# Two attention layers on one core: each row-maximum operation is declared to the planner as a writer of its whole accumulator bank, and the planner gets a new table of offsets

## The chip, the cores and the metric

The kernel runs on one core of one Trainium2 chip. The metric is device time in microseconds (us): the median of three runs of the kernel before is 1676.51 us (1674.89 to 1676.59).

## The reference

Two layers of the same size (sequence 2048, width 1024, 32 heads of 32) are computed in float32, and their outputs stand side by side. Layer A goes over four segments of 512 tokens. In each it does causal softmax attention inside the segment and reads a memory of the earlier segments; layer B is a linear attention with a learned feature map.

```python
# layer A, segment s (qs, ks, vs: heads x 512 x 32)
logits = einsum("bhqd,bhkd->bhqk", qs, ks) * scale + mask     # mask: -1e9 above the diagonal
a_dot = softmax(logits) @ vs
a_mem = phi(qs) @ M / (phi(qs) @ z + 1e-6)                    # phi(t) = t + 1 if t > 0 else exp(t)
outs.append(g * a_mem + (1 - g) * a_dot)
M, z = M + phi(ks)^T vs, z + sum(phi(ks))
a = concat_heads(outs) @ wo
# layer B
phi_x = concat(softmax(x @ w_phi), softmax(-x @ w_phi))       # for x = q and x = k
b = concat_heads(phi_q @ (phi_k^T v) / (phi_q @ sum(phi_k) + 1e-6)) @ wo
out = concatenate([a, b], axis=-1)
```

## The kernel before

Products that need float32 accuracy are made of three float16 products: each operand is split into a high and a low half, and high x high, high x low and low x high are accumulated in one bank of the accumulator memory (PSUM, eight banks of 128 x 512 float32).

**Attention (layer A, to about 880 us).** The work is cut into 32 units, u = 0 to 31: one segment and one group of four heads each. `produce(u)` projects keys, queries and values (PE, L496), splits them (ACT L938, DVE L940) and copies the halves by DMA into a tile `S` (three in turn). `attend(u)` then does the following.

- *Maxima.* For softmax a row maximum is needed for each of 4 heads h and 4 blocks i of 128 query rows. Block i sees 128·(i+1) keys, so the score products are 128 to 512 columns wide. `maxima` (L991 to L1007) takes a bank of kind `s`, has PE write the products of one or two blocks into it (L999), and has DVE add the causal mask and take the maximum over each block's columns (L1005, in the trace `CUSTOM_DVE_ANT_0` with an accumulator read behind it; the result lands in a column of `mt`). Per head, (h,3) has a bank of its own (512 columns), (h,2) and (h,0) share one (384 and 128 columns), and for each two heads (h−1,1) and (h,1) share one (256 and 256). That makes 16 maxima in 10 banks a unit, 512 in all.
- *Their way into the scores.* POOL makes `mh` and `mr` from all 16 columns of `mt` (L1020 to L1022), PE turns them into rows (L1024), ACT copies these (L1026), and DMAs put them into the tile `S` as eight extra rows, so that the second score product (L1104) comes out with the maximum taken off.
- *Softmax and output.* ACT takes the exponential and the high half (L1108, L1110), DVE the low half (`ph`, L1111), POOL masks (L1117), PE multiplies by the values (`pv`, L1140), DVE sums (`oall`, L1144) and scales, PE transposes (L1172), ACT copies (`oT`, L767).

Beside it the weights of layer B are folded (L1245, L1248) and split. **Layer B** follows with products by Strassen's method (L710), then the output projections (L496 and L1805).

**What sets the order.** Nothing is issued while the program's operations are named. Each is recorded with its engine, an assumed duration, a due time `prio`, and the tiles that it reads (`r`) and writes (`w`). A write can name a part of a tile by a key: `(ps, i)` is part i of the bank, `ps` alone is all of it. Two operations depend on each other if they touch the same part or if one touches the whole. The planner (`Graph.run`) then goes through an imagined time: it takes the engine that can start something first, and on it, among the operations whose dependencies are done at that moment, the one with the smallest due time. A dependency of DVE on DVE adds 0.13 us in that imagined time. What comes out is the order of the instructions on each engine; each engine runs its own in that order and waits on semaphores for the others. These waits come from the tiles that the instructions really touch, not from the keys.

`MOVES` is a table by engine. Operations named in a row with the same due time are a job, numbered from 0, and the table adds an offset to the due time of one engine's operations of one job:

```python
prio += MOVES.get(eng, {}).get(self.job[1], 0.0)
```

Of the kernel before, what the change touches and what calls it, by code (L numbers as in the profile page):

```python
# [383 lines left out]
def tile_kernel(ctx: ExitStack, tc: tile.TileContext, ax, aw, awv, awo, beta, bx, bwqk, bwv, bphi, bwo, out):  # L384
# [68 lines left out]
    for t in mhp:  # L453
# [9 lines left out]
       w=[gates], prio=0.2, lat=2.0, kb=16)  # L463
# [284 lines left out]
    def group(u):  # L748
# [4 lines left out]
       w=[(stk[0], (1, 3))], prio=0.3)  # L753
    for t in stk[1:]:
        op(SP, 0.6, lambda t=t: nc.sync.dma_start(t()[96:104, 1], stk[0]()[96:104, 1]), r=[(stk[0], (1, 3))],
           w=[(t, (1, 3))], prio=0.3, lat=1.6, kb=32)
# [213 lines left out]
    def attend(u):  # L970
# [18 lines left out]
        mt = G.buf("a", [128, 4, 4], F32, "mt", 2)  # L989

        def maxima(*blocks):  # L991
            ps = bank("s", [128, 512], "maxima")
# [43 lines left out]
        if s > 0:  # L1036
            amem = G.buf("a", [128, 4, 4, 32], F32, "amem", 1)
            for b in range(2):
                ps = bank("misc", [128, 2, 4, 33], "memory")
# [837 lines left out]
```

## Time and profile before

| | |
|---|---|
| median of three runs | 1676.51 us (1674.89 to 1676.59) |
| the profiled execution's own time | 1675.73 us |
| its span, first to last instruction | 1674.0 us |
| mean granted TensorE clock | 0.997 of full speed |
| instructions | 40119 |
| moved by DMA | 299.18 MB, mean 179 GB/s |

A row of the timeline has the start and the duration in us, then engine, line, operation and tiles (out<-in); what stands in brackets is the idle time before it and who ended it. Durations of products on PE overlap: the next product starts before the duration of the last is over, so the distance of two starts is what a product costs. The same holds for DVE, where the accumulator read behind a maximum starts before the maximum's duration is over. A row of waits has the engine and line that waited, whom it waited for, the sum in us, how often, and the longest.

### The profile page before, as it was taken

The page shows a single profiled execution, that of the slowest core. Times are in us where ns is not written, and L with a number is a line of the kernel's source. Part 1 is how long each engine was busy: PE and PEld are TensorE (multiplying, and loading weights), DVE is VectorE, ACT ScalarE, POOL GpSimd, SP SyncE. Part 2 cuts the span into 40 slices and gives each one's busy share as a digit, 9 for nine tenths or more (in the row PEclk, how much of TensorE's full clock was granted, in tenths as well). Part 3 has the DMA queues.
Part 4 walks back from the last instruction along what each step waited for, and adds up shares of the span by engine and source line. Part 5 has one row for each costly group of instructions (what it writes and reads, how often), then busy time and mean ns, then how long its engine had stood idle before and what let it go on. Part 6 is the DMA issues. An engine that isn't in the chain of part 4 may idle for free.

```text
span 1674.0 us, 40119 instructions
## 1 busy us (share of the span) xinstructions
PE 1633.2 (98%) x14964; PEld 963.1 (58%) x14964; DVE 1355.2 (81%) x3187; ACT 1120.9 (67%) x2096; POOL 1062.9 (63%) x1453
## 2 busy tenths in 40 slices
PE   8999999999999999999999999999979999999999
PEld 6666756766676676667665444445534444444444
DVE  6999899998998877798874898778999888964451
ACT  7789979795978878678744676766445555543341
POOL 4667878866689988778541767636478897730000
PEclk9999999999999999999999999999989999999999
DMA  6866765787866576755457364467546768872321
GB/s 211 224 175 151 250 185 169 226 212 191 229 166 210 154 197 210 200 172 157 104 159 274 123 223 164 154 219 283 195 101 166 182 171 183 212 181 99 108 88 69
DMA packets 291410, 299.18 MB, mean 179 GB/s; under 512 B 169088, under 2 KB 222336, under 8 KB 284560
## 3 DMA queue, kind: packets, MB, share of 16 engines
q1 hardware_dynamic: 291216, 296.63, 61.1%
q8 instruction: 117, 1.92, 0.5%
q14 instruction: 77, 0.63, 0.1%
HBM read 161.17 MB, written 86.05 MB: 148 GB/s over the span
## 4 chain that ended last, share of the span: by engine, by line
PE 43%; DVE 5%; ACT 1%; DMA 1%; POOL 0%; issue 0%; DVEq 0%; ACTq 0%
PE proj L710 17%; PE misc L496 9%; PE proj L1805 5%; PE s L710 3%; PE s L1805 2%; PE misc L710 2%; PE misc L1805 1%; PE kv L1556 1%; DVE mx L1395 1%; PE pv L1746 1%; DMA pt<-S 1%; DVE S L1734 1%; DVE pt L1549 1%; DMA wf_d<-oT 0%; DVE r L1405 0%; DVE s L1005 0%
## 5 line engine op out<-in xcount | busy, mean ns | idle before, releaser
L496 PE MATMUL proj<-S,S 128*128 128x128 f16 (+1 forms) x3072 | 500.5, 299 | 2.8 <-ACT S L529 1.2
L496 PEld LDWEIGHTS <-S 128*128 128x128 f16 x4608 | 327.7, 97 | 152.7 <-issue 9.8
L710 PE MATMUL proj<-S,S 128*128 128x512 f16 x1584 | 365.2, 380 | 3.9 <-ACT cs L716 2.4
L710 PEld LDWEIGHTS <-S 128*128 128x128 f16 x2016 | 192.5, 98 | 224.1 <-issue 7.8
L1111 DVE SCALAR_TENSOR_TENSOR ph<-s,ph 128x512 f16<-128x512 f32 x320 | 210.4, 682 | 50.6 <-ACT ph L1110 48.3
L1005 DVE CUSTOM_DVE_ANT_0 s<-s,causal 128x512 f32<-128x512 f32 (+3 forms) x512 | 240.9, 513 | 8.8 <-PE s L999 5.0
L1117 POOL TENSOR_SCALAR_AFFINE_SELECT ph<-ph 128x256 f16<-128x256 f16 (+1 forms) x448 | 195.1, 458 | 76.6 <-DVE ph L1111 58.5
L1110 ACT ACTIVATE ph<-s 128x512 f16<-128x512 f32 x320 | 191.9, 657 | 1.3 <-POOL fo L609 0.4
L496 PE MATMUL misc<-S,ot 128*128 128x512 f16 x768 | 172.2, 379 | 0.0
L1402 ACT ACTIVATE e<-e,sk 128x256 f32<-128x256 f32 x256 | 112.4, 496 | 67.0 <-DVE e L1399 64.2
L496 PEld LDWEIGHTS <-ot 128*128 128x128 f16 x768 | 73.5, 98 | 87.2
L1104 PE MATMUL s<-S 104*128 104x512 f16 (+3 forms) x512 | 117.0, 299 | 2.7 <-DVE amem L1049 0.7
L999 PE MATMUL s<-S 96*128 96x512 f16 (+3 forms) x512 | 111.2, 299 | 3.4 <-ACT pk L952 1.0
L1108 ACT ACTIVATE s<-s,os 128x512 f32<-128x512 f32 x160 | 105.7, 705 | 12.8 <-PE s L1104 12.7
L1108 ACT ACTIVATE s<-s,bd 128x512 f32<-128x512 f32 x160 | 108.0, 721 | 2.5 <-PE s L1104 2.4
L496 PE MATMUL proj<-wv,S 128*128 128x128 f16 x1536 | 108.2, 219 | 0.4 <-DVE ph L1111 0.4
L1140 PEld LDWEIGHTS <-ph 128*128 128x128 f16 x2560 | 87.8, 96 | 20.5 <-issue 2.8
L1140 PE MATMUL pv<-vl,ph 128*128 128x66 f16 (+1 forms) x2560 | 92.3, 184 | 1.5 <-ACT pk L952 0.7
L1405 DVE TENSOR_REDUCE r<-e 128x32 f32<-128x1024 f32 x64 | 76.7, 1207 | 18.0 <-ACT e L1402 17.9
L1710 POOL TENSOR_TENSOR e<-e,zb 128x512 f32<-128x512 f32 x62 | 82.5, 1350 | 12.4 <-ACT zb L1582 7.2
L1005 DVE DVE_READ_ACCUMULATOR2_ANT mt<- 128x1 f32 x512 | 72.4, 141 | 0.0
L1514 POOL TENSOR_TENSOR e<-e,r 128x1024 f32<-128x1024 f32 x32 | 62.1, 1943 | 14.4 <-DVE r L1408 10.0
(345 smaller groups left out, 3259.9 us busy)
## 6 DMA issues: line engine op xcount, KB each, us to landing
S<-xf_d SPq DMA_DIRECT2D x126, 256.0 KB
S<-h SPq DMA_DIRECT2D x192, 128.0 KB
S<-wf_d SPq DMA_DIRECT2D x21, 1024.0 KB
st<-bwqk SPq DMA_DIRECT2D x64, 256.0 KB
out<-os SPq DMA_DIRECT2D x40, 256.0 KB
S<-aw SPq DMA_DIRECT2D x16, 512.0 KB
wa_d<-S SPq DMA_DIRECT2D x16, 512.0 KB
wf_d<-fo SPq DMA_DIRECT2D x32, 256.0 KB
```

What stands on the lines that cost most here:

```text
L496: op(PE, dur, lambda c=c, a=a, b=b, lv=lv, rv=rv: nc.tensor.matmul(pv(), lv(), rv(), start=(c == 0 and a + b == 0), stop=(c == n - 1 and a ...
L710: op(PE, 0.215, lambda n=n, a=a, b=b, lv=lv, rv=rv: nc.tensor.matmul(ps(), lv(), rv(), start=(start and n == 0 and a + b == 0), stop=(n == ...
L999: nc.tensor.matmul(ps()[:, o:o + 128 * i + 128], st()[0:96, 0, h, 128 * i:128 * i + 128], st()[0:96, 1, h, 0:128 * i + 128], start=True, s ...
L1005: dve(0.073 + 0.001125 * n, lambda h=h, i=i, o=o, n=n: nc.vector.tensor_tensor_reduce(ps()[:, o:o + n], ps()[:, o:o + n], causal[:, 512 - ...
L1104: nc.tensor.matmul(ps()[:, o:o + n], st()[0:104, 1, h, 128 * j:128 * j + 128], st()[0:104, 0, h, 128 * j:512], start=True, stop=True)
L1108: act(0.59, lambda: nc.scalar.activation(ps(), ps(), AF.Exp, bias=0.0, scale=bdv()[:, 3, i2, 0:1]), r=[(bd, i2)], w=[ps])
L1110: act(0.48, lambda: nc.scalar.activation(ph()[:, 0], ps(), AF.Copy, scale=2.0 ** 14), r=[ps], w=[(ph, 0)])
L1111: dve(0.6, lambda: nc.vector.scalar_tensor_tensor(ph()[:, 1], ps(), 2.0 ** 14, ph()[:, 0], op0=OP.mult, op1=OP.subtract), r=[ps, (ph, 0)], ...
L1117: nc.gpsimd.affine_select(pd, pd, pattern=[[0, n], [1, 128]], compare_op=OP.is_ge, fill=0.0, base=0, channel_multiplier=-1)
L1140: nc.tensor.matmul(ps()[:, i, n0:n1], ph()[:, a, o:o + 128], vl()[:, j, h, n0:n1], start=(i == 0 and a == 0), stop=(j == min(i, 2)), skip_ ...
L1402: op(ACT, 0.41, lambda i=i: nc.scalar.activation(e()[:, 4 * i:4 * i + 4], e()[:, 4 * i:4 * i + 4], AF.Exp, bias=0.0, scale=sk()[:, i:i + 1 ...
L1805: op(PE, 0.215, lambda n=n, a=a, b=b: nc.tensor.matmul(ps(), v(a)[:, n, :], wform[w]()[:, b, n, :], start=(start and n == 0 and a + b == 0 ...
```

## The change

Each maximum is declared as a writer of `ps`, the whole bank, instead of part i of it. In the planner the second maximum of a bank thus depends on the first also where their numbers i differ: in 128 pairs, (h,2) and (h,0) of each head and unit. The pairs (h−1,1) and (h,1) had equal keys and depended on each other before. The table `MOVES` is replaced; a line of it is shown. For jobs above 209 only a few offsets differ. No operation, duration, tile or DMA is added or removed. The new table has one line fewer, so each line of the code behind it has a number smaller by one (L1005 is L1004).

```diff
 MOVES = {
     "DVE": {
-        0: -8.8, 4: -25.3, 7: 1.6, 8: -0.7, 10: -2.9, 12: -20.2, 13: 24.6, 14: -1.3, 15: -10.6, 16: -16.6, 17: 0.6, 18: 0.7,
...
+        0: 0.8, 4: -24.4, 8: 1.2, 9: -0.9, 10: -1.2, 12: -18.7, 13: 72.6, 14: 9.7, 16: 16.9, 17: 53.7, 18: 0.3, 19: 0.8,
...
                 dve(0.073 + 0.001125 * n, lambda h=h, i=i, o=o, n=n: nc.vector.tensor_tensor_reduce(
                     ps()[:, o:o + n], ps()[:, o:o + n], causal[:, 512 - n:512], 1.0, NEG, OP.add, OP.max,
-                    mt()[:, h, i:i + 1]), w=[(mt, (h, i)), (ps, i)])
+                    mt()[:, h, i:i + 1]), w=[(mt, (h, i)), ps])
```

The order moves on all engines: 6129 of PE's 9476 operations, 1705 of DVE's 2666, 1269 of ACT's 2011, 1003 of POOL's 1438 and 655 of SP's 1033 stand in another place than before. Two places show what moves.

DVE, the last maxima of unit u = 14, before. The first name is the bank (`s_` and its number), the last part the width; the row with `mt` alone is the accumulator read.

```order
L1005 ISA s_7306,mt_7225<-s_7306,causal_82 128x512
L1005 ISA mt_7225 128x1
L1005 ISA s_7321,mt_7225<-s_7321,causal_82 128x384
L1005 ISA mt_7225 128x1
L1005 ISA s_7321,mt_7225<-s_7321,causal_82 128x128
L1005 ISA mt_7225 128x1
L1005 ISA s_7333,mt_7225<-s_7333,causal_82 128x256
L1005 ISA mt_7225 128x1
L1005 ISA s_7333,mt_7225<-s_7333,causal_82 128x256
```

The same place with the change:

```order
L1004 ISA s_7819,mt_7751<-s_7819,causal_82 128x512
L1004 ISA mt_7751 128x1
L1004 ISA s_7813,mt_7751<-s_7813,causal_82 128x128
L1004 ISA mt_7751 128x1
L1004 ISA s_7828,mt_7751<-s_7828,causal_82 128x384
L1004 ISA mt_7751 128x1
L1004 ISA s_7865,mt_7751<-s_7865,causal_82 128x256
L1004 ISA mt_7751 128x1
L1004 ISA s_7828,mt_7751<-s_7828,causal_82 128x128
L1004 ISA mt_7751 128x1
L1004 ISA s_7865,mt_7751<-s_7865,causal_82 128x256
```

Before, the two maxima of a bank (384 and 128 wide of s_7321, 256 and 256 wide of s_7333) stand directly behind each other; now a maximum of another bank stands between them. Over the kernel, 105 of the 128 pairs (h,2), (h,0) and 3 of the 64 pairs (h−1,1), (h,1) stand directly behind each other before, and 2 and 0 with the change.

PE, just ahead of the product that turns the maxima of the same unit into rows (L1024 before, L1023 with the change), before. `proj` is a projection of a later unit.

```order
L496 LDWEIGHTS S10_5648
L496 MATMUL proj_7326<-S5_5604,S10_5648 128x512
L1024 LDWEIGHTS mh0_126
L1024 MATMUL misc_7369<-identr_89,mh0_126 128x128
L496 LDWEIGHTS S10_5648
L496 MATMUL proj_7326<-S5_5604,S10_5648 128x512
```

With the change:

```order
L495 LDWEIGHTS S10_5624
L495 MATMUL proj_7822<-S5_5209,S10_5624 128x512
L998 LDWEIGHTS S12_135
L998 MATMUL s_7907<-S12_135 128x256
L998 LDWEIGHTS S12_135
L998 MATMUL s_7907<-S12_135 128x256
L1023 LDWEIGHTS mh0_126
L1023 MATMUL misc_7910<-identr_89,mh0_126 128x128
```

Before, sixteen projection products stand between the unit's last maxima product and L1024. With the change nine projection products and eight maxima products of the next unit, 128 to 512 columns wide, stand there.

## Rows read from the trace of the kernel before

**Rows 1.** The page: busy us of each engine (share of the span) x instructions.

```profile
PE 1633.2 (98%) x14964; PEld 963.1 (58%) x14964; DVE 1355.2 (81%) x3187; ACT 1120.9 (67%) x2096; POOL 1062.9 (63%) x1453
```

**Rows 2.** Busy time by stretch (us): length, engines (x), clock, DMA; last L1005 alone.

```profile
0.00:41.00 41.00, 36.69 (x287) 27.81 (x287) 27.05 (x73) 29.49 (x49) 18.45 (x34) 1.00 0.68 208
...
41.00:880.00 839.00, 819.72 (x8893) 564.20 (x8894) 738.43 (x2132) 671.56 (x1237) 636.90 (x1003) 1.00 0.67 187
...
900.00:1290.00 390.00, 377.26 (x2777) 185.84 (x2776) 324.84 (x558) 235.44 (x482) 239.78 (x234) 0.99 0.58 188
...
1210.00:1240.00 30.00, 18.39 (x164) 7.85 (x164) 29.93 (x52) 13.99 (x29) 22.11 (x23) 0.84 0.47 98
...
1290.00:1674.00 384.00, 379.56 (x2841) 174.36 (x2839) 252.26 (x404) 169.39 (x302) 160.20 (x166) 1.00 0.53 144
...
41.00:880.00 839.00, 254.88 (x1024) 1.00 0.67 187
```

**Rows 3.** Waits of PE, 40 to 900 us: sum, times, longest.

```profile
PE misc L1024 <- POOL mh L1022: 3.6, 8, 1.2
...
PE misc L1024 <- DVE wgs L511: 0.9, 1, 0.9
...
PE s L999 <- DMA S<-h: 0.8, 1, 0.8
...
PE misc L881 <- DVE xam L575: 0.2, 1, 0.2
```

**Rows 4.** Timeline of DVE, the end of the maxima of unit u = 14.

```profile
403.76 0.14 DVE L1005 DVE_READ_ACCUMULATOR2_ANT mt<- 128x1 f32 x1
403.94 0.30 DVE L1005 CUSTOM_DVE_ANT_0 s<-s,causal 128x128 f32<-128x128 f32 x1
...
404.15 0.73 DVE L1005 CUSTOM_DVE_ANT_0 s<-s,causal 128x512 f32<-128x512 f32 x1
...
404.80 0.60 DVE L1005 CUSTOM_DVE_ANT_0 s<-s,causal 128x384 f32<-128x384 f32 x1
405.32 0.14 DVE L1005 DVE_READ_ACCUMULATOR2_ANT mt<- 128x1 f32 x1
405.49 0.30 DVE L1005 CUSTOM_DVE_ANT_0 s<-s,causal 128x128 f32<-128x128 f32 x1
...
405.71 0.46 DVE L1005 CUSTOM_DVE_ANT_0 s<-s,causal 128x256 f32<-128x256 f32 x1
406.09 0.14 DVE L1005 DVE_READ_ACCUMULATOR2_ANT mt<- 128x1 f32 x1
406.27 0.43 DVE L1005 CUSTOM_DVE_ANT_0 s<-s,causal 128x256 f32<-128x256 f32 x1
406.62 0.14 DVE L1005 DVE_READ_ACCUMULATOR2_ANT mt<- 128x1 f32 x1
```

**Rows 5.** Timeline of DVE, a pair of maxima with a small operation between.

```profile
106.43 0.60 DVE L1005 CUSTOM_DVE_ANT_0 s<-s,causal 128x384 f32<-128x384 f32 x1
...
106.94 0.22 DVE L1227 SCALAR_TENSOR_TENSOR twf<-twf,phs 128x1 f32<-128x1 f32 x1
107.12 0.30 DVE L1005 CUSTOM_DVE_ANT_0 s<-s,causal 128x128 f32<-128x128 f32 x1
```

**Rows 6.** Timeline of PE, u = 14: what follows its last maxima product, and L1024.

```profile
403.83 3.62 PE L496 MATMUL proj<-S,S 128*128 128x512 f16 x16
408.65 0.23 PE L1024 MATMUL misc<-identr,mh 128*128 128x128 f16 x1 [1.20 <-POOL mh L1022]
```

**Rows 7.** Timeline of POOL in the same place.

```profile
406.92 0.26 POOL L1020 TENSOR_SCALAR mh<-mt 128x16 f16<-128x16 f32 x1 [1.68 <-DVE mt L1005]
...
408.04 0.56 POOL L1022 TENSOR_TENSOR mh<-mr,mt 128x16 f16<-128x16 f32 x1
```

**Rows 8.** Timeline of PE, u = 4: what follows its last maxima product, and L1024.

```profile
141.26 0.38 PE L1104 MATMUL s<-S 104*128 104x256 f16 x2
...
145.03 0.23 PE L1024 MATMUL misc<-identr,mh 128*128 128x128 f16 x1 [0.39 <-POOL mh L1022]
```

217 rows, old and new, of the table MOVES are left out of this document.

## The prediction

> **What bounds the kernel now.** I read the page's busy shares first, then busy time by stretch, then the waits of PE, and last the timelines of single places. PE is busy 98% of the span and every other engine at most 81% [rows 1], so the end moves only where PE stands still. By stretch [rows 2], PE idles 839.00 − 819.72 = 19.3 us in the attention part from 41 to 880 us, 12.7 us between 900 and 1290 us, and 4.4 us after that. The offsets differ in the first part alone: the order of all engines is the same again for what ran behind 1067 us before. Of the 12.7 us, 11.6 lie between 1210 and 1240 us [rows 2], behind that point, where I expect no change. So at most 19.3 us can be won, and the question is who ends PE's waits there. The waits of PE between 40 and 900 us [rows 3] come to 17.7 us in 42 waits. The mh chain on POOL, which follows the maxima, ends 8 of them (3.6 us). DVE ends 26 (10.3 us; 20 lines, first and last shown). DMA ends 2 (1.2 us), ACT, PE and other POOL work the rest. DVE is the engine that PE waits for, and it is busy 738.43 of 839.00 us, 88%.
>
> **What the declaration changes: a wait of DVE for itself.** The timeline of DVE in unit u = 14 [rows 4] shows a cost which the planner of before does not know. A 384-wide maximum starts at 404.80, its accumulator read at 405.32, and the 128-wide maximum of the same bank only at 405.49: 0.69 us from start to start. Another 384-wide one at 106.43 [rows 5], followed by a small operation on another tile, lets that start at 106.94, 0.51 us after it. The difference is 0.18 us. The bank's second maximum waits for the write of the first; the last two (256 and 256 wide, 405.71 and 406.27) are 0.56 us apart for the same reason. In [rows 5] the small operation takes the place of the wait: the 128-wide maximum starts at 107.12, 0.18 us behind it, and waits no longer than without it. A longer operation in between covers the wait whole.
>
> Counted in the order, 105 of the 128 pairs (h,2), (h,0) and 3 of the 64 pairs (h−1,1), (h,1) stand directly behind each other before, and 2 in all after the change. So 106 waits go: 106 × 0.18 = 19.1 us of DVE's time. Other pairs of DVE operations in which the second needs the first and follows directly grow from 139 to 151: 12 × 0.18 = 2.2 us comes back. Net 16.9 us, 2% of the 839 us of that part. No operation is added or taken away on any engine, the DMAs included, so busy time elsewhere stays. None of this is PE's time. What PE sees of it is the sum.
>
> **Term 1, waits that DVE ends.** 26 waits, 10.3 us, 0.40 us each [rows 3]. The least saving, if the work ahead of each is short by one wait: 26 × 0.18 = 4.7 us. The most: all 10.3 us. A unit has four or five such waits (0.7 to 0.9 us), more than the mean wait; yet the maxima take 254.88 of DVE's 738.43 us [rows 2], about a third, so most waits have other work ahead. I take 6 us, near the lower end. The order adds to this: from a bank of maxima to the bank's next maxima PE has, by count at the spacing of its products, a median of 2.7 us of other work before and 3.0 after, and in the lowest tenth 1.8 and 2.2.
>
> **Term 2, the chain from the maxima to L1024.** Unit u = 14 shows it in full: the last maxima product leaves PE at 403.83 [rows 6], DVE works without a gap to 406.76 [rows 4], POOL makes mh from 406.92 to 408.60 [rows 7], and L1024 starts at 408.65, after 1.20 us of idle PE: 4.82 us from 403.83. Three of the self-waits lie behind 403.7, at 403.76, 405.32 and 406.09, and cost 0.53 us; without them the chain is 4.3 us. In unit u = 4 it is 3.8 us (141.26 to 145.03, PE idle 0.39) [rows 8]. But the new order also asks for more. The sixteen products that stood between the last maxima product and L1024 in u = 14 (3.62 us, [rows 6]) are nine now, with eight short ones of the next unit, about 3.0 us. Over the 32 units, 13 have 4.2 us or less in between after the change, with a mean of 3.6, and 8 before. At a chain of 3.8 us the shortfalls sum to 3.7 us, today's 3.6; at 4.3 us to 13 × 0.7 = 9.1 us, which is 5.5 more than today. Were the chain always under 3.0 us, the 3.6 us would all go. I take 0: the chain is shorter by about as much as its cover. The ends are −3.6 and +5.5.
>
> **Moved steps with no term.** SP issues the same DMAs in another order (655 of 1033 places differ). PE waited for a DMA 1.2 us in two waits, so between −1.2 and, if two more such come, +1.2 us; I take 0, since the largest single one was 0.8 us [rows 3]. The first 41 us hold 4.3 us of idle PE [rows 2], and the order differs there only from about 30 us on: 0. ACT and POOL do the same work and are busy 67% and 63% [rows 1]; where they are late, it is behind DVE or PE: 0.
>
> **Sum.** The profiled execution took 1675.73 us (span 1674.0, 1.7 us around it), 0.8 us under the median of 1676.51. 1675.73 − 6 + 0 = 1669.7 us; from the median it is 1670.5. I say 1670.
>
> **A rule against it.** The rows have a wait of 0.18 us between the two maxima of a bank [rows 4, 5]. By the Trainium skill, "VectorE: DVE Perf Modes", section "The DRAIN you can't avoid", a semaphore between chained DVE operations costs nothing extra, since the engine drains after every operation anyway (8 copies, the same time with and without). By that rule the interleaving is worth nothing and the time would be that of before; the trace disagrees, 0.69 against 0.51 us.
>
> **The rivals.**
> 1. *Hidden.* DVE gets 16.9 us back, but spends them as idle time: PE's waits move to POOL's and ACT's links of the same chains, and the order of PE has only as much slack as the planner thinks it needs. For it: the L1024 distances are shorter, and DVE idled 100 us of 839 already. Against it: 26 of 42 waits end with DVE. It gives −1 to +1, so 1675 to 1677. Chance 0.19.
> 2. *No cost to remove.* The wait of 0.18 us only shifts time that DVE would have lost anyway, the mechanism of the rule above. Then nothing is saved, 1675.7 us. [Rows 4] and [rows 5] speak against it on the same pair of widths. Chance 0.03. That the change does not do what it says is excluded by the count of 2 pairs left, and I give it 0.01 within the same bound.
> 3. *Slower, the cover of L1024 is gone.* The chain stays at 4.3 us, since an interposed 512-wide maximum (404.15 to 404.80, 0.65 us [rows 4]) delays the second maximum of a bank more than the wait of 0.18 us did; 13 units are short by 0.7 us, 9.1 us against 3.6, and the 26 other waits stay as they are: 1675.7 + 5.5 = 1681.2 us. It decides from a chain of 3.8 us on. For it: the distances. Against it: all maxima of a unit must be done before mh, so what stands between two of them is mostly work of the same unit that must be done anyway. Milder forms, with some saving of term 1, fill 1679.9 to 1681. Chance 0.21.
>
> **How the numbers follow.** About 0.2%, 3.4 us, is what a measurement of this kernel tells from no change: faster is below 1673.2, slower above 1679.9. My forecast, term 1 between 4.7 and 10.3 with term 2 between −3.6 and +2, has 0.56 and its own range 1662 to 1673. Rivals 1 and 2 have 0.23, rival 3 has 0.21. The lower end of the range is both terms at their best, 1675.7 − 10.3 − 3.6 = 1661.8; above it the range goes to 1680, which leaves about 0.12 beyond it and some 0.05 below.
>
> **What would show it.** In the profile after, L1005's line (now L1004) should have pairs 384 and 128 wide of one bank with another operation between, and DVE some 15 us less busy between 41 and 880 us. PE should idle about 13 us instead of 19.3 there, its waits by DVE sum to 4 or 5 us instead of 10.3, and its waits for mh to 2 to 5 us. The stretch from 1210 to 1240 us should keep its 11.6 us of idle PE. I am wrong if DVE's busy time does not fall, if it falls and PE's idle time between 41 and 880 us does not, or if the waits for mh go above 7 us.

## The result, and the profile after

The changed kernel takes 1680.07 us (median of 13 runs, 1677.05 to 1682.6) against 1676.18 us of the kernel before on the same chip (13 runs, 1673.29 to 1678.01): ratio 1.0023, 95% interval 1.0015 to 1.0031. It is slower by 0.23%. 1670 us was predicted, with faster as the likeliest case. The profiled execution took 1677.05 us, the lowest of the 13; a second one, of 1680.88 us, is used below where it matters.

Busy time of each engine on the page, which answers to [rows 1]:

```profile
PE 1632.0 (97%) x14964; PEld 963.1 (57%) x14964; DVE 1346.0 (80%) x3187; ACT 1119.7 (67%) x2096; POOL 1058.6 (63%) x1453
```

Busy time by stretch after the change (columns as in [rows 2]), the last row for the maxima's line, now L1004, alone:

```profile
0.00:41.00 41.00, 36.73 (x294) 27.44 (x295) 25.18 (x76) 30.61 (x51) 18.42 (x38) 1.00 0.70 227
41.00:390.00 349.00, 334.98 (x3568) 228.67 (x3567) 319.56 (x940) 287.38 (x529) 259.50 (x411) 1.00 0.69 193
390.00:880.00 490.00, 482.52 (x5321) 335.94 (x5319) 411.95 (x1190) 383.51 (x710) 373.61 (x590) 1.00 0.67 182
...
41.00:880.00 839.00, 817.50 (x8885) 564.61 (x8884) 731.51 (x2130) 670.89 (x1237) 633.11 (x999) 1.00 0.68 187
...
1210.00:1240.00 30.00, 18.35 (x167) 7.76 (x166) 29.93 (x51) 12.79 (x26) 22.08 (x23) 0.86 0.45 94
...
41.00:880.00 839.00, 241.49 (x1024) 1.00 0.68 187
```

Two of these stretches before the change:

```profile
41.00:390.00 349.00, 340.65 (x3720) 234.20 (x3721) 327.26 (x957) 295.87 (x543) 268.44 (x428) 1.00 0.71 198
390.00:880.00 490.00, 479.06 (x5174) 330.00 (x5173) 411.17 (x1176) 375.69 (x695) 368.47 (x576) 1.00 0.64 180
```

The maxima cost DVE 241.49 instead of 254.88 us [rows 2]: 13.4 us less, so the waits of a maximum for the one ahead of it are gone. PE's idle time between 41 and 880 us has nevertheless grown, from 19.3 to 839.00 − 817.50 = 21.5 us (23.3 in the second profile). And the total hides two opposite halves. From 41 to 390 us PE idles 14.0 instead of 8.4 us, from 390 to 880 us 7.5 instead of 10.9. The first 41 us and the stretch from 1210 to 1240 us stand as before (in the second profile the first 41 us hold 5.3 us of idle PE instead of 4.3).

Waits of PE between 40 and 900 us after the change, which answer to [rows 3]:

```profile
PE misc L1023 <- POOL mh L1021: 3.4, 7, 0.9
PE s L998 <- DVE ph L1110: 1.6, 3, 0.7
PE misc L1244 <- DMA st<-bwqk: 1.6, 1, 1.6
PE s L998 <- DVE mt L1004: 1.1, 3, 0.5
PE s L1103 <- DVE mt L1004: 1.0, 2, 0.7
...
PE s L998 <- DMA S<-h: 0.9, 1, 0.9
...
PE proj L495 <- DVE mt L1004: 0.7, 2, 0.4
...
PE misc L876 <- DVE mt L1004: 0.6, 1, 0.6
...
PE misc L1041 <- DVE mt L1004: 0.5, 1, 0.5
```

Over all rows of this view DVE ends 24 waits with 10.5 us; before it was 26 with 10.3. But they are others: those for the maxima themselves (`mt`, five rows here) went from 6 with 1.8 us to 9 with 3.9 us, and all nine lie before 390 us. The waits for mh are nearly as before, 3.4 against 3.6 us, and those for DMA grew from 1.2 to 2.5 us.

One such place shows what PE waits for. DVE of the changed kernel, about 232 to 238 us:

```profile
231.89 3.98 DVE L530 SCALAR_TENSOR_TENSOR S<-S,wgs,S 128x512 f16<-128x512 f32 x3
235.79 0.29 DVE L1004 CUSTOM_DVE_ANT_0 s<-s,causal 128x128 f32<-128x128 f32 x1
...
236.00 0.73 DVE L1004 CUSTOM_DVE_ANT_0 s<-s,causal 128x512 f32<-128x512 f32 x1
...
236.65 0.59 DVE L1004 CUSTOM_DVE_ANT_0 s<-s,causal 128x384 f32<-128x384 f32 x1
237.16 0.14 DVE L1004 DVE_READ_ACCUMULATOR2_ANT mt<- 128x1 f32 x1
237.16 0.46 DVE L1004 CUSTOM_DVE_ANT_0 s<-s,causal 128x256 f32<-128x256 f32 x1
...
237.55 0.33 DVE L1004 CUSTOM_DVE_ANT_0 s<-s,causal 128x128 f32<-128x128 f32 x1
```

PE at the same place:

```profile
234.32 1.28 PE L495 MATMUL proj<-wv,S 128*128 128x128 f16 x20
236.19 0.16 PE L876 MATMUL misc<-pr,one 128*128 128x2 bf16 x1 [0.59 <-DVE mt L1004]
236.84 0.72 PE L1041 MATMUL misc<-mem,pq 128*128 128x132 f32 x4 [0.49 <-DVE mt L1004]
237.99 3.28 PE L495 MATMUL proj<-S,S 128*128 128x512 f16 x8 [0.43 <-DVE mt L1004]
```

Every interposed maximum costs only its own time: the 384-wide one is followed after 0.51 us, the 256-wide one after 0.39 us (before 0.69 and 0.56 [rows 4]). But three splits of the folded weights (L530, 3.98 us) stand ahead of them on DVE. At 235.6 us (234.32 + 1.28) PE's next product finds no free bank, and PE then waits three times, 1.5 us in all, each time until a bank's last maximum is through. The third wait ends just after the 128-wide maximum of 237.55. This one shares a bank with a 384-wide one, and the 256-wide one between the two delays the bank's release: it takes 0.39 us where the wait of DVE for itself cost 0.18.

### The profile page after: what moved, and what is told of

Same layout as the page of the kernel before. It is cut to its first block, busy times and chain, and to the rows that moved or that the text cites. A ratio compares the mean times of both kernels' runs of the same rounds, so it can differ in the third digit from the quotient of the medians.

```text
span 1675.3 us, 40134 instructions
## 1 busy us (share of the span) xinstructions
PE 1632.0 (97%) x14964; PEld 963.1 (57%) x14964; DVE 1346.0 (80%) x3187; ACT 1119.7 (67%) x2096; POOL 1058.6 (63%) x1453
## 4 chain that ended last, share of the span: by engine, by line
PE 51%; DVE 11%; ACT 4%; POOL 4%; DMA 2%; issue 2%; SPq 0%; ACTq 0%; POOLq 0%; DVEq 0%
PE proj L709 16%; PE misc L495 9%; PE proj L495 7%; PE proj L1804 5%; PE s L709 3%; PE s L1804 2%; DVE s L1004 2%; PE misc L709 1%; PE s L998 1%; PE pv L1139 1%; DVE ph L1110 1%; PE misc L1804 1%; PE s L1103 1%; DVE mx L1394 1%; ACT ph L1109 1%
## 5 line engine op out<-in xcount | busy, mean ns | idle before, releaser
L495 PE MATMUL proj<-S,S 128*128 128x512 f16 (+1 forms) x3072 | 504.5, 299 | 3.5 <-ACT S L528 1.2
L495 PEld LDWEIGHTS <-S 128*128 128x128 f16 x4608 | 325.0, 97 | 147.1 <-issue 11.3
L1004 DVE CUSTOM_DVE_ANT_0 s<-s,causal 128x512 f32<-128x512 f32 (+3 forms) x512 | 234.7, 523 | 6.9 <-PE s L998 6.6
L495 PE MATMUL proj<-wv,S 128*128 128x128 f16 x1536 | 103.4, 219 | 0.0
L1709 POOL TENSOR_TENSOR e<-e,zb 128x512 f32<-128x512 f32 x62 | 82.0, 1342 | 11.6 <-ACT zb L1581 7.2
L1004 DVE DVE_READ_ACCUMULATOR2_ANT mt<- 128x1 f32 x512 | 73.6, 144 | 0.0
L998 PEld LDWEIGHTS <-S 96*128 96x128 f16 x512 | 46.9, 97 | 45.6 <-issue 8.0
```

The lines of the kernel that those rows point to most:

```text
L495: op(PE, dur, lambda c=c, a=a, b=b, lv=lv, rv=rv: nc.tensor.matmul(pv(), lv(), rv(), start=(c == 0 and a + b == 0), stop=(c == n - 1 and a ...
L998: nc.tensor.matmul(ps()[:, o:o + 128 * i + 128], st()[0:96, 0, h, 128 * i:128 * i + 128], st()[0:96, 1, h, 0:128 * i + 128], start=True, s ...
L1004: dve(0.073 + 0.001125 * n, lambda h=h, i=i, o=o, n=n: nc.vector.tensor_tensor_reduce(ps()[:, o:o + n], ps()[:, o:o + n], causal[:, 512 - ...
```

## The experiments

Each order was taken with the maxima of a bank directly behind each other and with something between them. Further kernels joined the two orders at a point of time, and two more changed the planner alone.

**e4_split: only the self-waits go.** The kernel before, with its declaration and its table. After planning, the second maximum of a bank is moved behind the next DVE operation, in 107 of the 108 pairs that stand directly behind each other.

```diff
             o.fn()
...
+        for x, y, z in zip(dve, dve[1:], dve[2:]):
+            if not (x.pair and y.pair and x.pair[0] is y.pair[0] and x.pair[1] == 2):
+                continue
...
+            del line[a]
+            line.insert(c, y)
+        for o in line:
+            o.fn()
```

> The order of before on every engine, except that where the two maxima of a bank stand directly behind each other on DVE, the second is moved behind the next DVE operation (107 of 108 such pairs). Table and declaration are those of before. Theory 1 (the self-wait of 0.18 us costs PE time, and it is the rest of the new order that loses): 1669 to 1672 us against 1676, PE idle in 41 to 880 us down from 19.3 to about 14. Theory 2 (DVE's time back does not reach PE): 1675 to 1677, DVE some 15 us less busy there, PE idle as before. Theory 3 (the operation in between delays the second maximum and with it the release of its bank, and PE waits for the bank): 1678 to 1682, with more PE waits for the maxima.

1669.39 us (5 runs) against 1675.73 of before: ratio 0.9962, interval 0.9949 to 0.9974, 6.3 us less. This is faster than both kernels. The page's busy times, and the stretch from 41 to 880 us:

```profile
PE 1628.8 (98%) x14964; PEld 962.9 (58%) x14964; DVE 1343.2 (81%) x3187; ACT 1117.9 (67%) x2096; POOL 1062.4 (64%) x1453
```

```profile
41.00:880.00 839.00, 823.29 (x8936) 568.35 (x8934) 729.88 (x2138) 677.40 (x1252) 637.77 (x1007) 1.00 0.68 189
```

PE idles 15.7 us there, 3.6 less than before, and its busy time over the whole span is 4.4 us less than in [rows 1]; the same products are done, so both are part of the gain (the two profiled executions lie 8.2 us apart, 1667.52 against 1675.73). What shortened PE's busy time isn't shown. PE's waits from 40 to 900 us have no row for mh any more (before 3.6 us). Those for `mt` went from 1.8 (6) to 4.2 us (12), and all that DVE ends from 10.3 to 11.5 us. So the self-waits are worth the size that term 1 gave, but what the list of waits shows of the gain came by way of the mh chain, which term 2 had put at 0, and not through the waits that DVE ends. That the two sizes agree is chance. The delayed release of a bank by what stands between its maxima exists, and is smaller than the gain.

**e5_join: the changed kernel with its self-waits back, and more of them.** The changed kernel's order, with 126 of the 128 pairs (h,2), (h,0) put directly behind each other again.

```diff
+            a, c = line.index(x), line.index(y)
...
+            dve = [o for o in line[a + 1:c] if o.eng == "DVE"]
+            if dve:
+                del line[c]
+                line.insert(a + 1, y)
```

> The order of the changed kernel on every engine, except that the second maximum of a bank, 128 wide, is moved forward to stand directly behind the first on DVE (126 of 128 pairs), so that it waits 0.18 us again. Theory 1: the changed kernel's 1680 plus 4 to 7, so 1684 to 1687. Theory 2: 1679 to 1681. Theory 3: 1674 to 1677, since the banks come free earlier.

1693.61 us (4 runs), ratio 1.0106 (1.0092 to 1.0119), above what any of the three theories gave. The two parts of the attention, and the two longest waits of PE from 40 to 900 us:

```profile
41.00:390.00 349.00, 329.77 (x3474) 222.54 (x3473) 321.13 (x925) 281.74 (x519) 254.05 (x405) 1.00 0.68 192
390.00:880.00 490.00, 476.94 (x5262) 331.65 (x5260) 419.10 (x1173) 381.77 (x707) 371.57 (x580) 1.00 0.64 176
```

```profile
PE misc L1042 <- POOL mh L1040: 6.8, 13, 1.3
PE s L1016 <- DVE mt L1022: 4.1, 13, 0.9
```

The edit did more than the kernel before has. In the changed order a 128-wide maximum often stood between the two 256-wide ones of a bank, as in the order shown for u = 14; with it moved forward, these two meet. In the instruction order of e5_join all 128 pairs (h,2), (h,0) and 51 of the 64 pairs (h−1,1), (h,1) stand directly behind each other, 179 in all, against 108 before, none in e4_split and 2 with the change. One of the 51, on DVE of e5_join, 0.56 us from start to start:

```profile
95.64 0.47 DVE L1022 CUSTOM_DVE_ANT_0 s<-s,causal 128x256 f32<-128x256 f32 x1
96.02 0.14 DVE L1022 DVE_READ_ACCUMULATOR2_ANT mt<- 128x1 f32 x1
96.20 0.43 DVE L1022 CUSTOM_DVE_ANT_0 s<-s,causal 128x256 f32<-128x256 f32 x1
```

With the second set of runs of the changed kernel (after_again, below), taken on the same chip together with these, the four kernels make a square (us; in brackets the pairs that stand directly behind each other):

| | directly behind each other | with something between | difference |
|---|---|---|---|
| order of before | 1675.73 (108) | 1669.39 (0) | −6.3 |
| order of the changed kernel | 1693.61 (179) | 1679.33 (2) | −14.3 |
| difference | +17.9 | +9.9 | |

Parting the pairs gains in both orders. The right column compares like with like: with the pairs parted in both, the new order costs 9.9 us, more than the parting gains in the old one. The 17.9 of the left column also holds 71 more pairs, so it is not a price of the order alone; at 0.06 to 0.08 us a pair (6.3 us for 107, 14.3 for 177) an estimate gives them 4 to 6 us of it.

**after_again: the changed kernel once more.** The same kernel, no edit, for a second profile.

> The changed kernel once more, for a second profile on the same chip as the others. All theories: 1678 to 1682. In its profile the time should be lost against before between 80 and 390 us, as in the first profile, where PE reached the same amount of work 8 us later than before at 385 us; if it is won and lost in other places, the places of the first profile are chance.

1679.33 us (11 runs), ratio 1.0023 (1.0014 to 1.0032). PE's waits from 41 to 390 us come to 12.7 us (27) against 12.9 (27) in the first profile and 7.8 (18) before; from 390 to 880 us to 8.7 against 6.7 and 9.9. The loss in the first part is in both profiles, and so is a smaller gain in the second part.

**h1_old_then_new, h2_new_then_old: which part loses.** The planner's choice is replaced by a list of the operations. The list of h1 has the order of before for its first 4860 of 16625 operations (about 394 us) and behind that the changed kernel's; h2 the other way round.

```diff
-            o = min(some, key=lambda x: x.prio)
+            o = self.ops[ORDER[count]]
```

> The order of before for the first 4860 of its 16625 operations (to about 394 us), then the rest in the order of the changed kernel. Theory A (the new order loses its time between 80 and 390 us, where two profiles show it 7 to 8 us behind before, and is better from 400 to 880 us, where they win 4 to 7 us back): 1676 minus 4 to 7, so 1669 to 1672 us. Theory B (what is won back late is only the echo of being late: whoever is behind finds its operands ready): 1675 to 1678.

> The other way round: the first 4860 operations of the changed kernel, then the rest in the order of before. Theory A: 1676 plus 7 to 8, so 1682 to 1685 us. Theory B: 1678 to 1681, as the changed kernel.

h1: 1678.06 us (12 runs), ratio 1.0014 (1.0005 to 1.0022), the upper end of its theory B. h2: 1692.62 us (4 runs), ratio 1.0101 (1.0086 to 1.0115), above both of its theories. Up to 390 us each behaves as its part: PE's waits are 7.5 us in h1 and 12.2 in h2, against 7.8 in before and 12.9 after. Behind 390 us both are worse than either kernel: 11.3 us in h1 and 15.4 in h2, against 9.9 in before and 6.7 and 8.7 in the changed kernel's two profiles. Of these, 3.6 and 3.7 us are one wait near the seam, ended at 396.9 us in h1 and at 405.0 in h2. In h1 and then in h2, from the waits of PE between 390 and 880 us:

```profile
PE s L1109 <- DMA S<-rw: 3.6, 1, 3.6
```

```profile
PE misc L1072 <- DMA pkt<-kh: 3.9, 2, 3.7
```

By these two waits, each order leaves its transfers in a state which the other does not continue. Up to 390 us the first part of the new order is the part that loses; but two halves of orders can't be added up, since the seam costs as much as what was to be measured.

**h3_old_new_split, h3b_old_longer: the best of both?** h1 with the pairs of before's part split as in e4_split, joined at 4860 operations; and the same joined at 6640 (about 542 us).

```diff
+            o = self.ops[ORDER[count]]
...
+        for x, y, z in zip(dve, dve[1:], dve[2:]):
```

> As the first of these (before's order to 394 us, then the changed kernel's), and in the part of before each pair of maxima of one bank that stands directly behind each other gets the next DVE operation between it. Theory A: some 5 us less than without the split, 1664 to 1667 us, faster than both kernels and than before with the split alone (1669). Theory B: 1669 to 1672.

> The order of before with split pairs for the first 6640 of 16625 operations (to about 542 us) and the changed kernel's order behind that; h3_old_new_split went to 4860 (394 us) and came to 1673.57. Theory (the seam costs about 6 us wherever it lies, and the changed kernel's order gains 2 to 4 us a few hundred us long): a smaller stretch is left to gain in, so 1672 to 1677 us. Rival (the seam at 394 us was an unlucky place, and its cost depends on which transfers are on their way): without it the split of before's part and the gain of the rest add up, 1664 to 1669 us, below e4_split's 1669.39.

1673.57 us (12 runs), ratio 0.9989 (0.9979 to 0.9999), and 1682.07 us (5 runs), ratio 1.0034 (1.0022 to 1.0047). Both came out above what either side had expected. The later seam has no long wait for a transfer (0.4 us in all from 390 to 880 us) but waits for the softmax, the three longest between 540 and 556 us; PE of h3b_old_longer, 41 to 880 us:

```profile
PE pv L1161 <- POOL ph L1138: 6.4, 2, 3.9
PE proj L516 <- DVE ph L1132: 5.3, 5, 4.1
```

Neither beats e4_split. What a seam costs depends on where it lies, and is not a constant 6 us.

**e7_split_all: other waits of DVE for itself.** e4_split, with 101 further pairs split, in which a DVE operation needs the one directly ahead of it.

```diff
+        for x, y, z in zip(dve, dve[1:], dve[2:]):
+            if not any(d is x and not k for d, k in y.deps) or line.index(y) < line.index(x):
+                continue
```

> Before's order with the split of the maxima pairs, and with the same done for 101 more pairs of neighbouring DVE operations in which the second needs the first. If every self-wait of DVE counts like those of the maxima (6.3 us for 107 of them): 1663 to 1666 us. If only those in the chain to the maxima's rows count: 1668 to 1670. If what is put between delays the others: 1671 to 1675.

1669.37 us (6 runs), ratio 0.9963 (0.9951 to 0.9974), the time of e4_split. DVE is 2.9 us less busy (1340.3 against 1343.2), and PE does not see it. But the edit parted less than it moved, since a moved operation can come to stand directly ahead of one that needs it. In the instruction order of e4_split 124 operations wait for a result of the DVE operation directly ahead, none of them a maximum, and in e7_split_all still 89: 35 fewer. At the price of the maxima's pairs, 6.3 us for 107, these would be worth 2 us (an estimate), and that is not seen. That only the waits inside the maxima pay is thus likely and not shown.

**e1_decl: the declaration under the old table.**

```diff
-                    mt()[:, h, i:i + 1]), w=[(mt, (h, i)), (ps, i)])
+                    mt()[:, h, i:i + 1]), w=[(mt, (h, i)), ps])
```

> The new declaration with the old table. If the new offsets fit the planner that knows of the dependency, and the old ones only the planner of before, this is slower than both, 1682 to 1700. If the loss lies in the new offsets, and the declaration itself is harmless or good, 1670 to 1677. On DVE 2 pairs stand directly behind each other, as in the changed kernel.

1762.92 us (4 runs), ratio 1.0521 (1.0507 to 1.0535): slower than both, as the first theory had it, but far above its 1700. The new table under the old declaration gives no kernel to compare: the planner comes to a point where no operation can start. So the share of the table alone stays unknown.

**e10_lat: one other number of the planner.**

```diff
-            ("DVE", "DVE"): 0.13, ("DVE", "PE"): 0.4, ("DVE", "POOL"): 0.16, ("PE", "ACT"): 0.4, ("PE", "DVE"): 0.2,
+            ("DVE", "DVE"): 0.14, ("DVE", "PE"): 0.4, ("DVE", "POOL"): 0.16, ("PE", "ACT"): 0.4, ("PE", "DVE"): 0.2,
```

> The kernel before with one number of the planner changed: a dependency of DVE on DVE is assumed to add 0.14 us instead of 0.13. Declaration, table, operations and DMAs are those of before; only the order that is planned differs. Theory A (the offsets of the table belong to one exact course of the planner, so any change to the planner gives another order, whose own waits are no longer those that the table was fitted to): well above before, over 1690 us, PE idle between 41 and 880 us above 30 us instead of 19.3; the loss in the changed kernel's first part is then of this kind, a new order with waits of its own, and not a consequence of the split pairs. Theory B (the order is robust, and what the changed kernel loses comes from the declaration, which puts other work between two maxima of a bank): 1673 to 1678 us, as before, PE idle 18 to 21 us.

1750.36 us (5 runs), ratio 1.0440 (1.0426 to 1.0455). The page's busy time of PE, the stretch from 41 to 880 us, and PE's longest waits from 40 to 900 us:

```profile
PE 1667.0 (95%) x14964; PEld 976.5 (56%) x14964; DVE 1365.5 (78%) x3187; ACT 1120.7 (64%) x2096; POOL 1063.1 (61%) x1453
```

```profile
41.00:880.00 839.00, 794.20 (x8322) 540.30 (x8323) 705.74 (x2007) 642.33 (x1183) 612.92 (x954) 0.96 0.65 177
```

```profile
PE s L999 <- DVE mt L1005: 6.4, 12, 2.4
PE s L1104 <- DVE ph L1111: 5.7, 9, 1.9
PE pv L1140 <- DVE ph L1111: 5.3, 7, 1.6
```

An assumed 0.01 us more, with the declaration and the table of before, costs 74 us (against 1676.85 on that chip). PE idles 44.8 instead of 19.3 us in that stretch, and over the whole span it is also busy 33.8 us longer, at a mean granted clock of 0.976 instead of 0.997; so waiting is only a part of the 74 us, and the lower clock is another; how much each is isn't measured. The declaration of e1_decl costs 87 us under the same table. So, by these two runs, a table holds for one exact course of the planner. The new table brought the new declaration's order back to within 4 us of before, but not to the level which the old order reaches with its pairs split.

**The first part, seen from DVE.** Groups of DVE's instructions between 41 and 390 us, before and then after (busy, mean ns, then idle time ahead of them and who ended it):

```profile
L1005 DVE CUSTOM_DVE_ANT_0 s<-s,causal 128x384 f32<-128x384 f32 (+2 forms) x224 | 105.6, 513 | 4.4 <-PE s L999 2.8
L1111 DVE SCALAR_TENSOR_TENSOR ph<-s,ph 128x512 f16<-128x512 f32 x120 | 78.7, 682 | 7.5 <-ACT ph L1110 7.2
...
L940 DVE SCALAR_TENSOR_TENSOR h<-proj,bd,h 128x512 f16<-128x512 f32 x27 | 19.9, 743 | 0.7 <-ACT h L938 0.4 <-ACT z L952 0.2
L531 DVE SCALAR_TENSOR_TENSOR S<-S,wgs,S 128x512 f16<-128x512 f32 x24 | 19.1, 844 | 0.4 <-ACT S L529 0.3
```

```profile
L1004 DVE CUSTOM_DVE_ANT_0 s<-s,causal 128x384 f32<-128x384 f32 (+3 forms) x224 | 103.1, 519 | 0.4 <-PE s L998 0.4
L1110 DVE SCALAR_TENSOR_TENSOR ph<-s,ph 128x512 f16<-128x512 f32 x113 | 74.4, 681 | 12.0 <-ACT ph L1109 12.0
...
L530 DVE SCALAR_TENSOR_TENSOR S<-S,wgs,S 128x512 f16<-128x512 f32 x24 | 22.3, 966 | 0.8 <-ACT S L528 0.8
L939 DVE SCALAR_TENSOR_TENSOR h<-proj,bd,h 128x512 f16<-128x512 f32 x28 | 20.9, 747 | 8.0 <-ACT z L951 3.4 <-ACT pq L951 1.6 <-DMA S<-awv 1.2
```

Before, DVE idles 4.4 us ahead of its maxima, mostly for PE's scores; with the change 0.4 us: the scores are nearly always there first and lie in their banks. In exchange DVE idles 8.0 instead of 0.7 us ahead of the halves of the projections (`h`) and 12.0 instead of 7.5 us ahead of `ph`, both times mostly for ACT, though it did seven `ph` fewer by 390 us. This fits a DVE that stands still for ACT while maxima follow behind, so that PE lacks banks; no run shows it by itself, and at the place shown at 232 us it was the splits that stood ahead.

## Why the prediction was wrong

- *The self-wait and its price* [rows 4, 5] were right. L1004 has the interleaved pairs. Over all 105 pairs of before the 128-wide maximum starts a median of 0.69 us behind its 384-wide one; with another maximum between, that one follows the 384-wide one after a median of 0.515 us in e4_split and in the changed kernel. e4_split moves the second maxima of 107 pairs and nothing else, and is 6.3 us faster. That term 1 says 6 us is luck: it took them from the waits that DVE ends, and in e4_split these rose from 10.3 to 11.5 us. The Trainium skill's sentence on chained operations ("VectorE: DVE Perf Modes", section "The DRAIN you can't avoid"), that the semaphore between them costs nothing extra, does not hold for two maxima of one bank: the 0.69 us are measured where the second waits for DVE's own semaphore. Rival 2 is thereby out.
- *DVE's busy time* was to fall by some 15 us between 41 and 880 us. The maxima's share fell by 13.4, but the whole only by 6.9 (738.43 to 731.51): other operations became longer, as the 24 splits L530 of 19.1 and then 22.3 us above.
- *The step that failed* is in term 1: "26 waits, 10.3 us", of which 6 were to go. It took the waits of the old order for those of the new one and subtracted. But the change plans anew: two thirds of PE's operations stand elsewhere, and the list has other waits, 24 with 10.5 us. With the pairs parted in both orders the new one costs 9.9 us. This term was missing; "moved steps" gave SP, ACT and POOL 0 us since they do the same work. Parting the pairs in the old order gives −6.3, the new order +9.9, together the +3.6 of the runs taken with the experiments (+3.9 in the first set).
- *Term 2* was right as taken, 0: the waits for mh are 3.4 us against 3.6. Its two halves show by themselves: with the pairs parted and the old cover the waits for mh are gone (e4_split, −3.6), and with the new cover and the pairs together they are 6.8 us (e5_join, with 71 pairs more than before). Rival 3 gave nearly the measured time, 1681.2, by a mechanism that did not come: L1023's cover held. Its side remark, that an interposed maximum delays the bank's release, is seen at 237 us, and the waits for `mt` rose from 6 to 9; how much of the loss that is isn't shown, as e4_split has 12 and is faster.
- *Rival 1* (DVE's time won, but spent as idle time on ACT's links) fits the first part best, with DVE's idle time ahead of `h` and `ph`; its price of −1 to +1 us was too small.
- *From 1210 to 1240 us* PE's 11.6 us of idle time stayed, 30.00 − 18.35 = 11.65, as said. The waits for DMA rose by 1.3 us, just over the bound of 1.2 (in the second profile by 0.4).
- The text's own conditions for being wrong were met: DVE's busy time fell, and PE's idle time rose from 19.3 to 21.5 us.

Open is which engine's moves before 390 us do the harm. The operations share eight banks, so one engine's order can't be exchanged alone, and it wasn't tried.

## What to carry to other kernels

Where a planner with fitted numbers sets the order, an edit of what it sees is two changes: the local effect, and a new order whose waits are not those of the old trace; the second needs a term of its own, as wide as the plan's own scatter (74 us here for a 0.01 us change of one latency, a part of it by the clock). A local gain is best taken by a move after planning that leaves the rest of the order alone: e4_split, 1669.39 us, beats both kernels. And two operations of DVE of which the second waits for the first, as these two maxima of one bank, should have another operation between them, if that does not hold up the bank's release where banks are short.

## What the hardware showed beyond that

The chained maxima touch different columns of their bank, and still the second starts 0.18 us later than an operation on another tile would; with an operation between them this is gone. The wait is one that the program puts in: the second maximum carries a wait for DVE's own semaphore, which the accumulator read behind the first one raises. What the trace shows of the chip is the price of that, 0.18 us; whether two maxima on different columns would need the wait, no run shows. And 35 waits fewer at other DVE operations changed nothing in the kernel's time (1669.37 against 1669.39 us).

Where PE stood still more, its granted clock fell too. In e10_lat it was 0.96 as a mean from 41 to 880 us, in e1_decl 0.94 from 390 to 880 us, the latter in this row:

```profile
390.00:880.00 490.00, 456.21 (x4646) 309.34 (x4647) 376.51 (x1093) 338.68 (x624) 332.44 (x511) 0.94 0.60 170
```

Before it was 1.00 in this stretch with 10.9 us of idle PE, here there are 33.8 us. A mean of 0.94 between the levels of 2.4 and 1.2 GHz is, by an estimate, about an eighth of the stretch at the lower one, so part of those 87 us is clock and not waiting. The changed kernel's clock is 1.00 in both parts, as before.
